# A list scheduler's cost figures are replaced, and with them the order of an attention and MoE kernel

## The chip, the cores and the metric

The kernel runs on one core of one Trainium2 chip. The metric is the device time of one execution in microseconds. A core has five engines that each take their instructions in the order in which the program lists them: TensorE (PE in the profile, its weight loads PEld), VectorE (DVE), ScalarE (ACT), GpSimd (POOL) and SyncE (SP), which here issues all DMAs. An instruction that needs a result of another engine waits for it, and everything behind it on its own engine waits too. So the order within each engine is part of the program.

## The reference

```python
scores = scale * np.matmul(q, k.transpose(0, 1, 3, 2))
log_f = np.log(np.clip(f, 0.0001, 1.0))
cum = np.cumsum(log_f, axis=-1)
decay = cum[:, :, :, None] - cum[:, :, None, :]
scores = np.where(causal, -1000000000.0, scores + decay)
scores = scores - np.max(scores, axis=-1, keepdims=True)
attn = np.exp(scores)
attn = attn / (np.sum(attn, axis=-1, keepdims=True) + 1e-09)
attn_out = np.matmul(attn, v)            # 8 batches, 8 heads, 576 rows, 64 columns
x = attn_out.transpose(0, 2, 1, 3).reshape(4608, 512)
h = np.maximum(np.maximum(x @ w1, x @ w2), x @ w3)      # 4608 x 768
out = h @ w_out                                          # 4608 x 512
```

All inputs are float32, but the kernel takes q, k, v and f as such and the four weight matrices as 64-bit numbers, which it converts on the chip.

## The kernel before

**Heads.** The 64 heads (8 batches of 8) go one after the other. Scores are held transposed, keys on the partitions. A head's 576 query columns are cut into unit 2 (columns 0 to 255) and unit 1 (columns 256 to 575); in the first batch unit 1 is cut again into "a" and "b". `scores(n, unit)` is a chain over four engines. A first pass of matmuls writes the scores into PSUM (banks `s`, L606). From head 16 on VectorE adds the causal mask (L635, L640). ScalarE copies the first block (L671), VectorE takes the maximum over the key blocks (`mx`, L659 to L664), GpSimd reduces it over the partitions (`gm`, L674) and writes the result into a row of the query tile (`qs_r`, L681). A second pass of matmuls (L606 again) adds minus that maximum and the low parts of q and k to the same banks. Then ScalarE takes the exponential (`pf`, L688).

**Split numbers.** To keep float32 accuracy at a faster matmul rate, each factor is split into a high part, rounded by ScalarE, and a low part, subtracted by VectorE. For the weights of the values these are `ph` (L694) and `pl` (L695), and `split_values` runs three groups of matmuls: `ph` with the high values, `ph` with the low ones, `pl` with the high ones (bank `t`, L709). The first batch works in plain float32 instead.

**MoE.** When a batch is done, its output is divided by the row sums, which go through DRAM, and split (`xh`, `xl`). For each of two column chunks (256 and 320 wide) and six blocks of 128 hidden units `gemm1` (L818) computes three products of 12 matmuls each; ScalarE copies the first into `tm` (L825), VectorE takes the maximum with the other two (L827), and the result is split into `hmh` and `hml`. `gemm2` (L847) multiplies with `w_out`. The matmuls of batch b's MoE are the work that fills TensorE while heads of batch b+1 wait for their maxima.

**Buffers.** There are two sets of query and key tiles, so head n+2's DMAs wait for head n's second pass; the PSUM has four banks for scores, one (`t`) for values and three (`mp`) for the MoE.

**The planner.** Nothing of this is issued as it is written. Each step is given to `add` with an engine, a cost in ns, its function, the keys it reads and writes, and a priority. `emit` then simulates the engines: at each moment the engine that can start first takes, of its steps whose inputs are ready, the one with the best rank (priority less a little for the length of work behind it). `LAG` is the time from one engine's end to another's start, a DMA's transfer is queued behind the others, and `GatedClock` gives TensorE half speed after a stretch of 3413 ns with too little work. The steps are then issued in the order of the simulated starts. So a cost that is too low lets the planner believe that a result is there early, and it places the consumer early on its engine.

**Start.** `warm_up` holds 20 matmuls on an identity matrix. Heads 0 and 1 are transposed by TensorE from tiles `hml` and `hmh` (`turn_head`, L432), the other heads of the first batch by VectorE in groups of four (`load_quad`, L491). The decay row of each head goes by a small DMA into the key tile. 24 weight blocks (`load_weights`, L468 to L478) are converted by ScalarE and VectorE in the first 170 us.

Of the kernel before, what the change touches and what calls it, by code (L numbers as in the profile page):

```python
# [23 lines left out]
class GatedClock:  # L24
# [24 lines left out]
class Plan:  # L49
# [8 lines left out]
    ENGINES = ("PE", "ACT", "DVE", "POOL", "SP")  # L58

# [22 lines left out]
    def emit(self):  # L82
# [22 lines left out]
        while done < n:  # L105
# [30 lines left out]
def mm_cost(cols, m):  # L136
    return max(cols / 2.4 + 3, 107 if m > 65 else 55)


def run_cost(cols):  # L140

    load = [m / 1.2 for _, m in cols[1:]] + [107]
    return sum(max(n / 2.4 + 3, x) for (n, _), x in zip(cols, load))
# [11 lines left out]
def kernel(  # L155
# [52 lines left out]
    plan.parts["pf1"] = [f"pf1/{x}" for x in range(3)]  # L208
    for c in ("mx", "gm", "sg"):
# [39 lines left out]
    NB32 = 1  # L249
    UT = [sb(f"u{i}", [P, S]) for i in range(KT)]  # L250
# [115 lines left out]

    def sums_constants():
# [9 lines left out]
    add("POOL", 1800, constants, w=["const"], prio=-9)  # L377
    add("POOL", 150, lambda: nc.gpsimd.memset(LESS.bitcast(F32), -1.0), w=["less"], prio=-9)
    for i in range(H):
        add("POOL", 480, lambda i=i: first_constants(i), w=[f"qf{i}/2"], prio=-9 + i)  # L380
        add("DVE", 369, lambda i=i: nc.vector.memset(KF[i][64:P, :], 0.0), w=[f"kf{i}/2"], prio=-9 + i)
    add("POOL", 1000, value_constants, w=[f"vn{i}" for i in range(4)], prio=-8)


    def decay():
# [16 lines left out]
        add("DVE", 369, lambda: nc.vector.tensor_scalar(c8, ft[0:H, :], -1.0 / scale, None, op0=ALU.mult),  # L402
# [599 lines left out]
```

## Time and profile before

| | |
|---|---|
| median of 3 runs | 991.08 us (990.32 to 992.14) |
| profiled execution | 992.66 us |
| its span, first to last instruction | 990.9 us |
| mean granted TensorE clock | 0.986 |
| DMA | 112.69 MB, mean 114 GB/s |

The page lists busy time per engine, the span in 40 slices of 24.8 us, and groups of equal instructions. A busy TensorE is counted from a matmul's start to its modelled end, so neighbouring matmuls overlap; the spacing of their starts is what one costs. In a row of the timeline stand the start, the length, engine, line, operation, out<-in, shapes, and in brackets the idle time before it and what ended that. A wait row names the engine and line that waited, what it waited for, the total in us, how often, and the longest. "First to second pass" below means the time from the first to the second group of L606 matmuls of one head and unit.

### The profile page before, as it was taken

The page shows a single profiled execution, that of the slowest core. Times are in us where ns is not written, and L with a number is a line of the kernel's source. Part 1 is how long each engine was busy: PE and PEld are TensorE (multiplying, and loading weights), DVE is VectorE, ACT ScalarE, POOL GpSimd, SP SyncE. Part 2 cuts the span into 40 slices and gives each one's busy share as a digit, 9 for nine tenths or more (in the row PEclk, how much of TensorE's full clock was granted, in tenths as well). Part 3 has the DMA queues.
Part 4 walks back from the last instruction along what each step waited for, and adds up shares of the span by engine and source line. Part 5 has one row for each costly group of instructions (what it writes and reads, how often), then busy time and mean ns, then how long its engine had stood idle before and what let it go on. Part 6 is the DMA issues. An engine that isn't in the chain of part 4 may idle for free.

```text
span 990.9 us, 18561 instructions
## 1 busy us (share of the span) xinstructions
PE 947.8 (96%) x6694; PEld 879.9 (89%) x6694; DVE 678.9 (69%) x1355; ACT 513.0 (52%) x1066; POOL 278.7 (28%) x314
## 2 busy tenths in 40 slices
PE   7999897999999999999999999999999999999998
PEld 4789786998989989899999989898998989899998
DVE  8789898687776785758757686667767686543211
ACT  3476556666555564546545654546555564433111
POOL 5553305233232323233213232323232323210000
PEclk9799799999999999999999999999999999999999
DMA  7882664645444452526354343435445352400000
GB/s 208 197 232 46 169 182 97 179 102 162 111 130 118 106 149 70 152 59 165 90 155 119 92 135 84 135 82 156 108 97 152 81 141 67 119 13 35 1 32 22
DMA packets 97258, 112.69 MB, mean 114 GB/s; under 512 B 54048, under 2 KB 63520, under 8 KB 97168
## 3 DMA queue, kind: packets, MB, share of 16 engines
q1 hardware_dynamic: 97168, 111.52, 42.9%
q8 instruction: 53, 0.87, 0.4%
q14 instruction: 37, 0.30, 0.1%
HBM read 50.15 MB, written 9.86 MB: 61 GB/s over the span
## 4 chain that ended last, share of the span: by engine, by line
PE 64%; DVE 14%; POOL 10%; DMA 5%; issue 4%; SPq 2%; ACT 1%; POOLq 0%; DVEq 0%; ACTq 0%
PE mp L818 35%; PE s L606 10%; PE mp L847 9%; PE t L709 8%; POOL gm L674 6%; DVE mx L664 4%; POOL qs_r L681 3%; DVE hl L491 2%; DMA hl<-in_k_dram 2%; DVE pl_r L695 2%; SPq L533 1%; DMA ks_r<-hl 1%; DVE tm L827 1%; DVE s L635 1%; PE mp L606 1%
## 5 line engine op out<-in xcount | busy, mean ns | idle before, releaser
L818 PE MATMUL mp<-xh_r,w_r 128*128 128x320 f32 (+1 forms) x2160 | 462.7, 297 | 0.6 <-DVE tm L827 0.6
L818 PEld LDWEIGHTS mp<-xh_r,w_r 128*128 128x128 f32 x2160 | 356.7, 188 | 2.5 <-DVE tm L827 1.6
L674 POOL PARTITION_ALL_REDUCE gm<-mx x131 | 172.9, 1323 | 579.2 <-DVE mx L664 363.2
L818 PE MATMUL mp<-xl_r,w_r 128*128 128x320 f32 (+1 forms) x1080 | 319.5, 296 | 0.0
L818 PEld LDWEIGHTS mp<-xl_r,w_r 128*128 128x128 f32 x1080 | 203.2, 188 | 0.3
L827 DVE TENSOR_TENSOR tm<-mp,tm 128x256 f32<-128x256 f32 (+1 forms) x192 | 87.1, 454 | 154.0 <-PE mp L818 131.2
L688 ACT ACTIVATE pf<-s 128x384 f32<-128x384 f32 (+4 forms) x251 | 113.7, 505 | 99.8 <-PE s L606 85.3
L606 PE MATMUL s<-qs_r,ks_r 128*128 128x320 f32 (+4 forms) x784 | 132.5, 290 | 24.9 <-POOL qs_r L681 18.8
L606 PEld LDWEIGHTS s<-qs_r,ks_r 128*128 128x128 f32 (+1 forms) x784 | 114.7, 182 | 44.0 <-POOL qs_r L681 32.2
L695 DVE TENSOR_TENSOR pl_r<-pf,ph_r 128x1216 fp32r<-128x1216 f32 (+1 forms) x112 | 113.1, 1011 | 23.7 <-ACT ph_r L694 23.1
L847 PE MATMUL mp<-w_r,hmh_r 128*128 128x512 f32 (+1 forms) x396 | 123.0, 392 | 0.7 <-DVE w_r L478 0.7
L694 ACT ACTIVATE ph_r<-pf 128x1216 fp32r<-128x1216 f32 (+1 forms) x112 | 97.5, 873 | 24.3 <-PE t L709 23.2
L830 ACT ACTIVATE hmh_r<-tm 128x256 fp32r<-128x256 f32 x96 | 39.8, 415 | 129.0 <-DVE tm L827 129.0
L664 DVE TENSOR_TENSOR mx<-mx,s 128x320 f32<-128x320 f32 (+3 forms) x248 | 92.1, 371 | 9.1 <-ACT mx L671 1.9
L491 DVE STREAM_TRANSPOSE hl<-hl 128x576 f32<-128x576 f32 x64 | 75.7, 1245 | 12.5 <-DMA hl<-in_k_dram 12.5
L847 PEld LDWEIGHTS mp<-w_r,hmh_r 128*128 128x128 f32 x396 | 71.0, 189 | 13.0 <-DVE w_r L478 1.0
L681 POOL CAST qs_r<-gm 1x320 fp32r<-1x320 f32 (+1 forms) x112 | 75.2, 674 | 6.9
L847 PE MATMUL mp<-w_r,hml_r 128*128 128x512 f32 (+1 forms) x198 | 77.1, 389 | 0.0
L709 PE MATMUL t<-ph_r,va_r 128*65 128x64 f32 x392 | 61.8, 274 | 2.4 <-ACT r_r L768 1.9
L709 PE MATMUL t<-pl_r,va_r 128*65 128x64 f32 x392 | 61.3, 272 | 1.6 <-DVE pl_r L695 1.3
L709 PE MATMUL t<-ph_r,vl_r 128*65 128x64 f32 x392 | 61.6, 273 | 0.0
L825 ACT ACTIVATE tm<-mp 128x256 f32<-128x256 f32 (+1 forms) x96 | 39.4, 410 | 42.0 <-PE mp L818 40.3
(186 smaller groups left out, 1150.3 us busy)
## 6 DMA issues: line engine op xcount, KB each, us to landing
qs_r<-hl SPq DMA_DIRECT2D x168, 144.0 KB
ks_r<-hl SPq DMA_DIRECT2D x168, 144.0 KB
hl<-in_q_dram SPq DMA_DIRECT2D x16, 576.0 KB
hl<-in_k_dram SPq DMA_DIRECT2D x16, 576.0 KB
w<-in_moe_w_dram SPq DMA_DIRECT2D x18, 512.0 KB
out_dram<-o_r SPq DMA_DIRECT2D x35, 256.0 KB
r_r<-rdram SPq DMA_DIRECT2D x56, 144.0 KB
vn<-in_v_dram SPq DMA_DIRECT2D x58, 128.0 KB
```

Source lines behind the costliest of these rows:

```text
L491: add("DVE", 669, lambda e=e, tt=tt, xs=xs: nc.vector.transpose(tt[:, e], xs[:, e]), [key + "0"], [key + "1"], prio)
L606: nc.tensor.matmul(bank[bk][0:l.shape[-1], col:col + w], l, rhs(qa, w), start=start and bk not in begun, stop=stop, skip_group_check=True)
L664: nc.vector.tensor_tensor(mt[:, a:a + w], mt[:, a:a + w], bank[bk][:, col:col + w], op=ALU.max)
L674: add("POOL", 185 + 3.43 * nq, lambda: nc.gpsimd.partition_all_reduce(gm, mt, P, bass.bass_isa.ReduceOp.max), [km, km + "a"], [kg], prio)
L681: add("POOL", 100 + 0.83 * nq, lambda: nc.gpsimd.tensor_copy(shift_row(), gm[row:row + 1, :]), [kg], [kx], prio)
L688: add("ACT", act_cost(w), lambda bk=bk, w=w, col=col: nc.scalar.activation(pf[:, col:col + w], bank[bk][:, 0:w], AF.Exp, scale=sc), [kb[bk ...
L694: add("ACT", act_cost(PW[unit]) + 40, lambda: nc.scalar.activation(ph(unit), pf, AF.Copy), [fk], [hk], prio)
L695: add("DVE", dve_cost(PW[unit]), lambda: nc.vector.tensor_tensor(pl(unit), pf, ph(unit).bitcast(F32), op=ALU.subtract), [fk, hk], [lk], prio)
L709: nc.tensor.matmul(t[:D + 1, qa:qa + w], src()[:, j, c, :], pr()[:, col:col + w], start=first and x == 0, stop=last, skip_group_check=True,)
L818: nc.tensor.matmul(m, unit_w(i, fb)[:, w, kt, :], xx, start=kt == 0 and x == 0, stop=kt == KT - 1 and x == 2,)
L827: add("DVE", dve_cost(cn), lambda m=m: nc.vector.tensor_tensor(t, m, t, op=ALU.max), [km, kt_], [kt_], prio)
L847: nc.tensor.matmul(mp[:, 0:cn], l[:, fb, cs], unit_o(fb)[:, r, ds], start=fb == 0 and x == 0, stop=fb == FT - 1 and x == 2,)
```

## The change

Most of the figures that the planner works with are replaced; `LAG` stays. TensorE's cost per column goes from 1/2.4 to 0.4477 ns and is then taken times 0.95; ScalarE and VectorE steps get 30 ns each, GpSimd steps 450 ns, and a DMA's landing 400 ns of room. The two limits of the clock model move. Costs of single steps follow: a memset 605 instead of 369, a transpose 1085 instead of 669, the reduction over partitions 450 + 2.6 instead of 185 + 3.43 ns per column, its copy 130 + 0.9 instead of 100 + 0.83. The warm-up matmuls write the bank `s10` (`SP1[0]`) instead of `mp2`. The keys of the value tiles are cut into three. A new set of functions for heads in plain float32 between `H * NB32` and `NV32` comes along, but `NV32` is set to `H`, so no head takes that way; only `second_constants`, four memsets on GpSimd ahead of the second batch, runs.

```diff
-        self.warm = share > (0.4 if self.warm else 0.65)
+        self.warm = share > (0.34 if self.warm else 0.72)
...
+    ROOM = {"PE": (0.95, 0), "ACT": (1.0, 30), "DVE": (1.0, 30), "POOL": (1.0, 450), "SP": (1.0, 0)}
+    LATE = 400
...
-            end = t + self.steps[i][1]
+            cost = self.steps[i][1] * self.ROOM[e][0] + self.ROOM[e][1]
+            end = t + cost
             if e == "PE":
-                end = clock.run(t, self.steps[i][1], self.steps[i][6])
+                end = clock.run(t, cost, self.steps[i][6])
...
-                end = moved = max(moved, end + 650) + self.steps[i][5]
+                moved = max(moved, end + 650) + self.steps[i][5]
+                end = moved + self.LATE
...
 def mm_cost(cols, m):
-    return max(cols / 2.4 + 3, 107 if m > 65 else 55)
+    return max(0.4477 * cols + 3, 107 if m > 65 else 55)
...
+    for i in range(2):
+        plan.parts[f"va{i}"] = [f"va{i}/{x}" for x in range(3)]
...
+    NV32 = H
...
+    def second_constants():
+        for i in range(2):
+            nc.gpsimd.memset(VF(i)[64:P, :, 4, :], 0.0)
+            nc.gpsimd.memset(VF(i)[:, :, :, D:D + 1], 1.0)
...
-        add("DVE", 369, lambda i=i: nc.vector.memset(KF[i][64:P, :], 0.0), w=[f"kf{i}/2"], prio=-9 + i)
+        add("DVE", 605, lambda i=i: nc.vector.memset(KF[i][64:P, :], 0.0), w=[f"kf{i}/2"], prio=-5.5 + 0.1 * i)
...
-            add("PE", 217, lambda: nc.tensor.matmul(MPS[2].rearrange("p (o x) -> p o x", o=4), ident, z, start=True, stop=True),
-                ["const"], ["mp2"], 90)
+            add("PE", 217, lambda: nc.tensor.matmul(SP1[0].rearrange("p (o x) -> p o x", o=4), ident, z, start=True, stop=True),
+                ["const"], ["sp1/0"], 90)
...
-                add("DVE", 669, lambda e=e, tt=tt, xs=xs: nc.vector.transpose(tt[:, e], xs[:, e]),
+                add("DVE", 1085, lambda e=e, tt=tt, xs=xs: nc.vector.transpose(tt[:, e], xs[:, e]),
...
-        add("POOL", 185 + 3.43 * nq, lambda: nc.gpsimd.partition_all_reduce(
+        add("POOL", 450 + 2.6 * nq, lambda: nc.gpsimd.partition_all_reduce(
...
-        add("POOL", 100 + 0.83 * nq, lambda: nc.gpsimd.tensor_copy(
+        add("POOL", 130 + 0.9 * nq, lambda: nc.gpsimd.tensor_copy(
...
-    add("POOL", 200, split_constants, w=["va0", "va1", "vl"], prio=p)
+    add("POOL", 1200, second_constants, w=["va0", "va1"], prio=p)
...
+        if n == NV32:
+            add("POOL", 1000, split_constants, w=["va0", "va1", "vl"], prio=p)
```

The figures act through the order alone, so it is shown at three places. Lines in the change are numbered by its own file: L671, L688, L694, L825 of before are L707, L725, L731, L868 there.

ScalarE, head 47, unit 1, from the copy of the first block of its maxima (`mx`, in the chain between the passes) to its first exponential (`pf<-s_123`, behind the second pass). Before:

```order
L671 ACTIVATE mx_82<-s_124 128x320
L694 ACTIVATE ph_r<-pf_80 128x1216
L766 ACTIVATE u_90<-t 64x320
L768 ACTIVATE r_r<-t 1x320
L688 ACTIVATE pf_81<-s_126 128x384
L825 ACTIVATE tm_121<-mp_130 128x320
L694 ACTIVATE ph_r<-pf_81 128x384
L766 ACTIVATE u_90<-t 64x256
L768 ACTIVATE r_r<-t 1x256
L688 ACTIVATE pf_80<-s_123 128x512
```

The change:

```order
L707 ACTIVATE mx_82<-s_124 128x320
L873 ACTIVATE hmh_r<-tm_121 128x256
L873 ACTIVATE hdh_r<-tm_121 128x64
L868 ACTIVATE tm_122<-mp_130 128x320
L547 ACTIVATE va_r<-vn_75 128x10x64
L517 ACTIVATE hl<-hl 128x1152
L806 ACTIVATE u_91<-t 65x320
L806 ACTIVATE u_91<-t 65x256
L868 ACTIVATE tm_121<-mp_130 128x320
L517 ACTIVATE hl<-hl 128x1152
L873 ACTIVATE hmh_r<-tm_122 128x256
L725 ACTIVATE pf_80<-s_123 128x512
```

Before, one MoE result (`tm`) is copied between the two; in the change two are, with 36 matmuls of TensorE from one to the next, and the high parts of the head before (`ph_r`) have moved ahead of the copy.

ScalarE again, from head 47's first exponential to its high part. Before:

```order
L688 ACTIVATE pf_80<-s_123 128x512
L688 ACTIVATE pf_80<-s_124 128x384
L688 ACTIVATE pf_80<-s_125 128x320
L495 ACTIVATE hl<-hl 128x1152
L830 ACTIVATE hmh_r<-tm_121 128x256
L830 ACTIVATE hdh_r<-tm_121 128x64
L495 ACTIVATE hl<-hl 128x1152
L825 ACTIVATE tm_122<-mp_130 128x320
L517 ACTIVATE va_r<-vn_75 128x10x64
L830 ACTIVATE hmh_r<-tm_122 128x256
L830 ACTIVATE hdh_r<-tm_122 128x64
L694 ACTIVATE ph_r<-pf_80 128x1216
```

The change:

```order
L725 ACTIVATE pf_80<-s_123 128x512
L725 ACTIVATE pf_80<-s_124 128x384
L725 ACTIVATE pf_80<-s_125 128x320
L725 ACTIVATE pf_81<-s_126 128x384
L731 ACTIVATE ph_r<-pf_80 128x1216
```

Eight other steps stood between the exponentials and the high part; in the change it is one, the exponential of the head's unit 2.

SyncE at the start; `hml` and `hmh` receive head 1's raw keys and queries, `qs`, `ks`, `xh`, `xl` the decay rows. Before:

```order
L336 DMA w_97<-in_moe_w_dram 128x4x256
L336 DMA qs_65<-u_91 1x16x36
L336 DMA qs_66<-u_91 1x16x36
L336 DMA ks_67<-u_91 1x16x36
L336 DMA ks_68<-u_91 1x16x36
L336 DMA xh<-u_91 1x16x36 x2
L336 DMA xl<-u_91 1x16x36 x2
L336 DMA hml<-in_k_dram 96x6x64
L336 DMA hmh<-in_q_dram 96x6x64
```

The change:

```order
L353 DMA w_97<-in_moe_w_dram 128x4x256
L353 DMA hml<-in_k_dram 96x6x64
L353 DMA hmh<-in_q_dram 96x6x64
L353 DMA qs_65<-u_91 1x16x36
L353 DMA qs_66<-u_91 1x16x36
L353 DMA ks_67<-u_91 1x16x36
L353 DMA ks_68<-u_91 1x16x36
```

The two raw loads have moved ahead of the eight decay rows. On TensorE head 1's transposes have likewise moved ahead of head 0's first scores.

More of the change, by code (lines that the diff above doesn't have):

```diff
@@ L136, in mm_cost @@
 def mm_cost(cols, m):
-    return max(cols / 2.4 + 3, 107 if m > 65 else 55)
+    return max(0.4477 * cols + 3, 107 if m > 65 else 55)
 def run_cost(cols):
     load = [m / 1.2 for _, m in cols[1:]] + [107]
-    return sum(max(n / 2.4 + 3, x) for (n, _), x in zip(cols, load))
+    return sum(max(0.4477 * n + 3, x) for (n, _), x in zip(cols, load))
 def act_cost(cols):
@@ L208 @@
     plan.parts["pf1"] = [f"pf1/{x}" for x in range(3)]
+    plan.parts["ph1"] = [f"ph1/{x}" for x in range(3)]
+    plan.parts["ph2"] = ["ph2/0"]
     for c in ("mx", "gm", "sg"):
@@ L282, in VA, with VF @@
         return lazy(f"va{i}", [P, 2, 5, D + 1])
+    def VF(i):
+        return lazy(f"va{i}", [P, 2, 5, D + 1], F32, "f")
     def VL():
@@ L315, in pl, with pg @@
         return lazy(f"pl{u}", [P, PW[u]])
+    def pg(u):
+        return lazy(f"ph{u}", [P, PW[u]], F32, "f")
     def unit_w(i, fb):
@@ L401, in decay @@
         c8 = UT[KT - 1][0:H, :]
-        add("DVE", 369, lambda: nc.vector.tensor_scalar(c8, ft[0:H, :], -1.0 / scale, None, op0=ALU.mult),
+        add("DVE", 540, lambda: nc.vector.tensor_scalar(c8, ft[0:H, :], -1.0 / scale, None, op0=ALU.mult),
             ["pf1"], [f"u{KT - 1}"], DP)
@@ L506, in load_v @@
         vn, kv = VN[i], f"vn{i}"
+        if NB32 * NP <= pi < NV32 // 2:
+            for j in range(2):
+                add("SP", 475, lambda j=j: nc.sync.dma_start(
+                    out=VF(s)[:, j, 0:4, 0:D], in_=src[j, 0:512, :].rearrange("(c p) d -> p c d", p=P)),
+                    [], [f"va{s}/{j}"], prio, 262144 / 360)
+            add("SP", 475, lambda: nc.sync.dma_start(
+                out=VF(s)[0:64, :, 4, 0:D], in_=src[:, 512:S, :].rearrange("h p d -> p h d")), [], [f"va{s}/2"], prio, 300000 / 360)
+            return
         after = [f"kf{2 * pi}"] if b < NB32 else []
@@ L574, in buffers @@
     def buffers(n, unit):
-        return SETS[n % len(SETS) if n < H * NB32 else 0] if unit == 2 else BUFS[unit]
+        if n < H * NB32:
+            return SETS[n % len(SETS)] if unit == 2 else BUFS[unit]
+        bufs = SETS[0] if unit == 2 else BUFS[unit]
+        if n < NV32 and n % 2:
+            bufs = bufs[:3] + (None,) + bufs[4:]
+        return bufs
     def scores(n, unit, prio):
@@ L646, in scores @@
             cost[run] = run_cost(ws)
-            ca = sum(4 * w / 2.4 for w, _ in ws) if first else cost[run]
+            ca = sum(4.04 * w / 2.4 for w, _ in ws) if first else cost[run]
             ca += 65 * mask_pe * sum(x[0] in run for x in diag)
@@ L666, in scores @@
         by_act = n < 0 if unit == 2 else True
-        cm = sum(dve_cost(x[1] * x[4]) for x in d["first"] if not (x[4] == 1 and by_act)) + sum(
+        cm = sum(dve_cost(x[1] * x[4]) + 110 * (x[4] == 3) for x in d["first"] if not (x[4] == 1 and by_act)) + sum(
             dve_cost(x[1]) + 128 for x in d["more"]) - 128 * (by_act and bool(d["more"]))
```

45 lines of the change are left out of this document (26 added, 19 removed).

## The prediction

> **What bounds the kernel now.** I read the page first, then the stretches of the span, then TensorE's waits by stretch, and last one head in order of time.
>
> ```profile
> PE 947.8 (96%) x6694; PEld 879.9 (89%) x6694; DVE 678.9 (69%) x1355; ACT 513.0 (52%) x1066; POOL 278.7 (28%) x314
> PEclk9799799999999999999999999999999999999999
> ```
>
> TensorE is busy for 947.8 of 990.9 us, so 43 us of idle time are all that an order can win, and besides them the slices near the start whose clock digit is 7. The stretches (columns: window, length, busy us of PE, PEld, DVE, ACT, POOL, then granted clock, DMA share, GB/s) show three stages.
>
> ```profile
> 0.00:25.00 25.00, 17.86 (x102) 12.10 (x103) 22.18 (x40) 9.01 (x16) 14.30 (x37) 0.99 0.74 210
> 25.00:100.00 75.00, 72.80 (x500) 64.80 (x500) 65.68 (x122) 46.91 (x107) 35.25 (x51) 0.91 0.62 158
> 100.00:175.00 75.00, 64.83 (x438) 57.49 (x436) 65.19 (x119) 44.41 (x90) 22.00 (x22) 0.91 0.54 146
> 175.00:875.00 700.00, 679.82 (x4901) 638.32 (x4900) 495.33 (x1005) 385.97 (x789) 205.74 (x202) 1.00 0.45 118
> 875.00:991.00 116.00, 112.49 (x763) 107.20 (x761) 30.56 (x74) 26.73 (x65) 1.46 (x2) 1.00 0.06 19
> ```
>
> Up to 175 us VectorE is busy for 153 us, TensorE for 155.5: a start-up in which either can be late. From 175 to 875 VectorE has 200 us to spare, and TensorE idles for 20.2 us. The last stretch is matmuls alone, and its 3.5 us are the final store. The middle stage's waits (us in total, times, longest), for matmuls and then for weight loads:
>
> ```profile
> PE s L606 <- POOL qs_r L681: 17.3, 31, 1.4
> PE s L606 <- DMA qs_r<-hl: 0.7, 1, 0.7
> PE t L709 <- DVE pl_r L695: 0.2, 1, 0.2
> ```
> ```profile
> PEld s L606 <- POOL qs_r L681: 29.0, 42, 1.7
> ```
>
> One cause holds nearly all of it: the second score pass waits for GpSimd, which reduces the row maxima over partitions (L674) and writes them into the query tile (L681). Head 47, later columns, shows the whole chain:
>
> ```profile
> 631.27 0.88 PE L606 MATMUL s<-qs_r,ks_r 128*128 128x320 f32 x5
> 632.17 0.42 DVE L635 TENSOR_TENSOR s<-s,mask 128x256 f32<-128x256 f32 x1
> 633.24 1.26 DVE L491 STREAM_TRANSPOSE hl<-hl 128x576 f32<-128x576 f32 x1 [0.65 <-DMA hl<-in_k_dram]
> 634.34 1.64 DVE L664 TENSOR_TENSOR mx<-mx,s 128x320 f32<-128x320 f32 x4
> 635.90 1.42 DVE L695 TENSOR_TENSOR pl_r<-pf,ph_r 128x1216 fp32r<-128x1216 f32 x1
> 636.15 2.27 POOL L674 PARTITION_ALL_REDUCE gm<-mx  x1 [2.63 <-DVE mx L664]
> 637.72 0.31 PE L818 MATMUL mp<-xh_r,w_r 128*128 128x320 f32 x1
> 638.49 0.87 POOL L681 CAST qs_r<-gm 1x320 fp32r<-1x320 f32 x1
> 639.41 0.91 PE L606 MATMUL s<-qs_r,ks_r 128*128 128x320 f32 x5 [1.38 <-POOL qs_r L681]
> ```
>
> From the first pass's end, 632.15, to the second's start, 639.41, the chain takes 7.3 us; the last matmul placed between them starts at 637.72. Both GpSimd steps are late against the stage's means:
>
> ```profile
> L674 POOL PARTITION_ALL_REDUCE gm<-mx x101 | 138.9, 1378 | 485.1 <-DVE mx L664 308.2 <-DVE mx L661 129.6 <-PE s L606 19.5
> L681 POOL CAST qs_r<-gm 1x320 fp32r<-1x320 f32 x51 | 33.4, 655 | 3.3
> ```
>
> **The change, part by part.** No instruction of TensorE, VectorE, ScalarE or the DMA queue is added or taken away; only the planner's figures change, and with them the order on each engine. So I add up waits.
>
> *The POOL waits of the middle stage.* What decides is how much other TensorE work stands between a head's first and second pass: I call it the cover. I counted it in both orders for all heads 14 to 63 and both column parts, pricing each matmul by the trace's spacing:
>
> ```profile
> 633.45 0.46 PE L818 MATMUL mp<-xh_r,w_r 128*128 128x320 f32 x2
> 633.74 0.31 PE L818 MATMUL mp<-xl_r,w_r 128*128 128x320 f32 x1
> 633.89 0.45 PE L818 MATMUL mp<-xh_r,w_r 128*128 128x320 f32 x2
> ```
>
> Three 320-wide matmuls start in 0.44 us, 147 ns each. For head 47's later columns 45 matmuls stand between the passes before (5.9 us) and 71 in the change (9.5 us; 48 of them 320-wide, 7.1 us). Over the 50 heads the later columns go from a mean of 5.9 to 8.9 us, smallest 7.6 from head 16 on; the first 256 columns from 5.4 to 9.4, smallest 7.7. The chain needs 7.3 us when as late as in head 47. Without the transpose that ran ahead of the maxima (1.26) and with GpSimd near its means (2.27 to 1.38, 0.87 to 0.66) it is 4.9. So almost every cover now exceeds the chain, with some 4 us over the usual one. What a stall costs lies between the two wait rows: in head 47 the matmul before started at 637.72, the next could at 637.87 and did at 639.41, a loss of 1.54 between 1.38 and 1.65, the latter being what the load row counts. I take 26 of the 29.0 for all, and leave 2 for the few covers that a very late GpSimd step eats: **-24**, bounds -15 (17.3 less 2) and -29.
>
> *What the cover is taken from.* The second pass now stands nearer to the weighted values. For the later columns the cover from the second pass to the first value matmul falls from a mean of 14.9 to 3.6 us (smallest 2.8), and to the matmuls that need the low part from 16.7 to 5.2 (smallest 4.6). The need, from head 47:
>
> ```profile
> 640.10 1.31 ACT L688 ACTIVATE pf<-s 128x512 f32<-128x512 f32 x3 [3.03 <-PE s L606]
> 640.16 0.31 PE L818 MATMUL mp<-xh_r,w_r 128*128 128x320 f32 x1
> 634.98 0.49 ACT L688 ACTIVATE pf<-s 128x384 f32<-128x384 f32 x1
> 635.37 0.43 ACT L825 ACTIVATE tm<-mp 128x320 f32<-128x320 f32 x1
> 648.38 1.22 ACT L694 ACTIVATE ph_r<-pf 128x1216 fp32r<-128x1216 f32 x1 [0.34 <-PE t L709]
> ```
>
> TensorE goes on at 640.16; the exponentials end at 641.41, 1.25 later. The changed ScalarE order puts the other part's exponential next (0.39, start to start) and then the high part (1.22): 2.9 us, against 3.6. VectorE's 1.42 for the low part makes 4.3, against 5.2. It fits with 0.7 to 0.9 to spare, and with nothing at the smallest covers. I take **+3**, 0.06 per head; bounds 0 and +10, which is 0.2 us in each of 50 heads.
>
> *The start-up.* Two effects meet. Head 1's raw keys and queries leave ahead of the eight decay rows instead of behind them:
>
> ```profile
> 10.15 1.22 SPq L336 DMA_DIRECT2D qs<-u  x2
> 14.04 0.89 PE L606 MATMUL s<-qs 128*128 128x256 f32 x4 [0.54 <-ACT qs L439]
> 15.27 0.52 SPq L336 DMA_DIRECT2D hml<-in_k_dram  x1
> 18.07 1.20 PE L432 MATMUL mp<-tm,hml 96*64 96x96 f32 x12 [0.53 <-DMA hml<-in_k_dram]
> ```
>
> The rows wait for their data until 10.15, so two issues ahead of them (0.52 for the first, the second alike) cost nothing. In the trace the load was issued at 15.27 and its transposes ran 2.8 us later; issued some 5 us earlier, behind the first weights, it lets them run at about 13 (an estimate from this distance). But TensorE's order now puts them ahead of head 0's scores, which started at 14.04. The warm-up matmuls write another bank, so the fourth transpose of head 0 stands with the other three; the 20 warm-ups cost what they did. Then VectorE sets the pace: priced by the trace, its steps up to those that head 11 needs are 9.7 us more than TensorE's work up to there before, 9.1 in the change. That floor stays. What can move is VectorE's own idle time, 22 us of the first 175. I take **-2**, bounds -12 (half of it) and +10 (as much lost again).
>
> The clock is part of it. Its rows:
>
> ```profile
> 100.00:125.00 25.00, 20.60 (x128) 18.32 (x126) 21.64 (x44) 14.11 (x29) 7.75 (x10) 0.80 0.62 172
> 103.31 0.28 PE L818 MATMUL mp<-pl_xa,w_r 128*128 128x256 f32 x1
> 105.74 0.65 PE L606 MATMUL s<-qs_r,ks_r 128*128 128x320 f32 x4 [2.15 <-issue]
> ```
>
> A pause of 2.15 us is followed by a clock of 0.80 over this stretch; over 25 to 175 us it is 0.91, 13.5 us lost. I keep that loss, for the floor keeps the pauses. The Trainium skill, "TensorE: Matmul & The Clock Gate", section "HAM oscillation — how this bites in real kernels", puts the limit at pauses of more than about 3.4 us. By that rule a start-up with pauses like this one's would run at full clock; the rows above say otherwise, and the sum goes by them.
>
> *Nothing.* `second_constants` adds four memsets on GpSimd. The nearest rows are of the same sizes, 0.20 and 0.12:
>
> ```profile
> 3.45 0.20 POOL L359 MEMSET vn<- 64x130 f32 x1
> 3.71 0.12 POOL L360 MEMSET vn<- 128x10 f32 x1
> ```
>
> Together 0.64 us at the start of batch 1, behind a wait for head 7's values that GpSimd already had there; if uncovered, head 8 waits 0.64.
>
> **Sum:** -24 + 3 - 2 = -23 us on a span of 990.9, so 968. The profiled execution took 992.66 in all, 1.76 around its span; the median of the runs is 991.08. I predict the median: **968 us**. The corners are 991 - 41 = 950 and 991 + 5 = 996.
>
> **The rivals.**
>
> *A, start-up gains too (955).* VectorE's idle time closes and head 1 is early: -12 more. For: 22 us of VectorE idle; against: the floor of 9 us is as before.
>
> *B, full clock in the start-up (954).* If only long pauses bring half speed, the 13.5 us go as well. For: the stage is a chain of pauses below 2.2 us; against: its clock is 0.91. The skill's page named above is this rule.
>
> *C, half of the POOL waits stay (980).* The chain grows with the cover: both parts' reductions now follow each other on GpSimd, and VectorE may put more work ahead of the maxima. The transpose in head 47 shows how. Against: it would take 4 us in every other head. -24 becomes -12.
>
> *D, the start-up loses (982).* Head 0's scores stand behind head 1's transposes and weights come later; +14 by the bound above and some clock.
>
> *E, slower (about 1000).* The place is the value matmuls of the later columns. ScalarE and VectorE run behind by more than the 0.7 to 0.9 us left, in every head, because each high or low part sits behind one more step (0.43 for a copy, 1.26 for a transpose). Against -26 elsewhere it decides from 26/50 = 0.52 us of wait per head on; at 0.7 it is +35, less 26: 1000. For: the high part was late before as well, at 648.38, seven us after its exponentials. Against: that was its place in the order.
>
> *F, no change (991).* The orders differ but the waits return in the same sum. Against: no cover of the 100 is now below the usual chain.
>
> **Numbers.** Forecast 0.50 (own range 960 to 976), A 0.13, B 0.03, C 0.14, D 0.10, E 0.07, F 0.03. The range 953 to 984 leaves out E, F and tails of the others. This kernel tells 0.2%, 2 us, from nothing. Faster: forecast, A, B, C and nearly all of D, 0.89; same 0.04, F and a rest; slower 0.07, E.
>
> **What would show it.** Right: between 175 and 875 us TensorE idles for 4 us or less, the rows "PE s <- POOL qs_r" come to under 3 us, and "PE t" waits for VectorE or ScalarE appear, small. First step wrong: those POOL rows stay above 8 us. Second: the "PE t" rows pass 10 us. Third: at the start of head 16's scores the changed kernel is over 8 us ahead or behind once the POOL waits are set aside. A clock below 1.00 after 200 us would upset all of it.

## The result and the profile after

The changed kernel takes 960.04 us (median of 4 runs, 958.37 to 960.95), the kernel before 990.7 us beside it: a ratio of 0.969, 95% interval 0.967 to 0.972. The forecast was 968 us with a range of 953 to 984. The profiled execution took 958.37 us in all, with a span of 956.6 against 990.9.

The page of the changed kernel, busy time and the clock's slices:

```profile
PE 931.5 (97%) x6694; PEld 879.2 (92%) x6694; DVE 674.3 (70%) x1355; ACT 501.4 (52%) x1066; POOL 253.2 (26%) x318
PEclk7999999999999999999999999999999999999999
```

The stretches of the changed kernel (window, length, busy us and count of PE, PEld, DVE, ACT, POOL, then clock, DMA share, GB/s):

```profile
0.00:25.00 25.00, 18.79 (x103) 14.11 (x104) 19.36 (x36) 8.33 (x14) 12.92 (x35) 0.80 0.75 211
25.00:100.00 75.00, 66.76 (x464) 58.98 (x463) 69.99 (x124) 45.40 (x102) 36.78 (x52) 0.93 0.72 189
100.00:175.00 75.00, 69.44 (x512) 64.85 (x511) 67.25 (x123) 48.91 (x101) 24.86 (x30) 0.95 0.45 125
175.00:875.00 700.00, 698.37 (x5085) 666.53 (x5085) 500.63 (x1033) 384.33 (x814) 178.60 (x204) 1.00 0.46 118
875.00:957.00 82.00, 78.18 (x540) 74.72 (x538) 17.11 (x42) 14.46 (x37) 0.00 (x0) 1.00 0.06 20
```

The middle stage shows the gain. In the same 700 us TensorE starts 5085 matmuls instead of 4901 and idles for 1.6 us instead of 20.2. The 184 more are 25 us of work at 698.37/5085 = 0.137 us each. Up to 175 us it has done 1079 instead of 1040, some 6 us. What is left behind 875 us takes 82 us instead of 116. GpSimd needs less time in the stage as well: 178.60 us instead of 205.74 for the same kind of work. The traces show where. The row of the copies before gives shortest, median and longest (ns):

```profile
L681 POOL CAST qs_r<-gm x101: 396/450/1507, 177.4 to 868.9; 1x320 fp32r<-1x320 f32 x51, 1x256 fp32r<-1x256 f32 x50
```

Of these 101 copies 20 run mostly beside VectorE's subtraction for the low part (`pl_r`, L695) and take 0.87 to 1.50 us each; the 15 that run beside no VectorE step take 0.40 to 0.45. In the change none of the 102 copies runs mostly beside that subtraction, and of the reductions 10 do instead of 25 (1.6 to 1.85 us each in the change, against 1.06 to 1.14 with VectorE idle). No run changes this alone.

The waits of that stage, matmuls and then weight loads (us in total, times, longest):

```profile
PE mp L861 <- DVE tm L870: 1.3, 1, 1.3
```
```profile
PEld mp L861 <- DVE tm L870: 1.5, 1, 1.5
PEld t L746 <- DVE pl_r L732: 0.6, 2, 0.4
PEld s L642 <- POOL qs_r L717: 0.3, 1, 0.3
```

The query row, for which weight loads waited 29.0 us in 42 places, is waited for once, 0.3 us. The value matmuls (`t`) wait for 0.6 us.

Head 47 again, GpSimd and then TensorE's passes, in order of time:

```profile
633.12 1.40 POOL L710 PARTITION_ALL_REDUCE gm<-mx  x1 [8.65 <-DVE mx L700]
634.90 1.63 POOL L710 PARTITION_ALL_REDUCE gm<-mx  x1 [0.38 <-PE t L746]
636.60 0.80 POOL L717 CAST qs_r<-gm 1x320 fp32r<-1x320 f32 x2
```
```profile
628.02 0.99 PE L642 MATMUL s<-qs_r,ks_r 128*128 128x320 f32 x7
638.24 0.99 PE L642 MATMUL s<-qs_r,ks_r 128*128 128x320 f32 x7
```

The rows of the two parts are now written together (x2), behind both reductions, and end at 637.40. The second pass starts at 638.24 with no idle time ahead of it, 0.84 us later. Before, it started at 639.41 after waiting 1.38 us.

### The profile page after: what moved, and what is told of

Same layout as the page of the kernel before. It is cut to its first block, busy times and chain, and to the rows that moved or that the text cites. A ratio compares the mean times of both kernels' runs of the same rounds, so it can differ in the third digit from the quotient of the medians.

```text
span 956.6 us, 18333 instructions
## 1 busy us (share of the span) xinstructions
PE 931.5 (97%) x6694; PEld 879.2 (92%) x6694; DVE 674.3 (70%) x1355; ACT 501.4 (52%) x1066; POOL 253.2 (26%) x318
## 4 chain that ended last, share of the span: by engine, by line
PE 86%; DVE 3%; DMA 1%; ACT 1%; issue 1%; SPq 0%; DVEq 0%; ACTq 0%
PE mp L861 47%; PE mp L890 15%; PE t L746 14%; PE s L642 10%; DVE pl_r L732 1%; DMA rdram<-sc 0%; DVE mx L700 0%; DMA r_r<-rdram 0%; DVE hl L519 0%; PE t L782 0%; DMA ks_r<-hl 0%; DMA qs_r<-hl 0%; ACT pf L725 0%; DVE ph L778 0%; PE s L658 0%
## 5 line engine op out<-in xcount | busy, mean ns | idle before, releaser
L861 PE MATMUL mp<-xh_r,w_r 128*128 128x320 f32 (+1 forms) x2160 | 475.7, 298 | 1.5 <-DVE tm L870 1.3
L710 POOL PARTITION_ALL_REDUCE gm<-mx x131 | 165.5, 1289 | 586.1 <-DVE mx L700 531.9
L725 ACT ACTIVATE pf<-s 128x384 f32<-128x384 f32 (+2 forms) x251 | 108.8, 508 | 69.0 <-PE s L642 63.7
L642 PE MATMUL s<-qs_r,ks_r 128*128 128x320 f32 (+4 forms) x784 | 120.8, 283 | 3.9 <-DMA ks_r<-hl 2.4
L731 ACT ACTIVATE ph_r<-pf 128x1216 fp32r<-128x1216 f32 (+1 forms) x112 | 97.1, 887 | 3.7 <-PE t L746 3.5
L868 ACT ACTIVATE tm<-mp 128x256 f32<-128x256 f32 (+1 forms) x96 | 39.7, 414 | 60.0 <-PE mp L861 57.5
L676 DVE TENSOR_TENSOR s<-s,mask 128x64 f32<-128x64 f32 x48 | 11.3, 235 | 80.8 <-PE s L642 80.6
```

The lines of the kernel that those rows point to most:

```text
L642: nc.tensor.matmul(bank[bk][0:l.shape[-1], col:col + w], l, rhs(qa, w), start=start and bk not in begun, stop=stop, skip_group_check=True)
L710: add("POOL", 450 + 2.6 * nq, lambda: nc.gpsimd.partition_all_reduce(gm, mt, P, bass.bass_isa.ReduceOp.max), [km, km + "a"], [kg], prio)
L725: add("ACT", act_cost(w), lambda bk=bk, w=w, col=col: nc.scalar.activation((pg(unit) if pk else pf)[:, col:col + w], bank[bk][:, 0:w], AF. ...
L731: add("ACT", act_cost(PW[unit]) + 40, lambda: nc.scalar.activation(ph(unit), pf, AF.Copy), [fk], [hk], prio)
L861: nc.tensor.matmul(m, unit_w(i, fb)[:, w, kt, :], xx, start=kt == 0 and x == 0, stop=kt == KT - 1 and x == 2,)
```

## Experiments

For the runs below I use three numbers per head and part, as means over heads 14 to 63. The **need** is the time in the trace from the end of the first pass to the end of GpSimd's copy of that head's row. The **cover** is the work placed between the passes, counted in the order and priced as in the prediction. The **margin** is cover minus need. "Load waits" are the waits of TensorE's weight loads. Each ratio is to the kernel before on the same chip, with its 95% interval.

### Which figures make the gain

*The GpSimd figures alone, on the kernel before.*

```diff
-            end = t + self.steps[i][1]
+            end = t + self.steps[i][1] + (450 if e == "POOL" else 0)
-        add("POOL", 185 + 3.43 * nq, lambda: nc.gpsimd.partition_all_reduce(
+        add("POOL", 450 + 2.6 * nq, lambda: nc.gpsimd.partition_all_reduce(
-        add("POOL", 100 + 0.83 * nq, lambda: nc.gpsimd.tensor_copy(
+        add("POOL", 130 + 0.9 * nq, lambda: nc.gpsimd.tensor_copy(
```

> The kernel before with the change's GpSimd figures alone: 450 + 2.6 and 130 + 0.9 ns per column, and 450 ns of room for each GpSimd step. Theory (the cover between the passes makes the gain, and the GpSimd figures make the cover): counted in its order, the covers of heads 14 to 63 have means of 7.0 us (first 256 columns) and 7.7 (later columns) against 5.4 and 5.9 before and 9.4 and 8.9 in the change. With needs of 4.3 and 5.65 us, the two that reproduce the waits of before, only 0.1 us is missing in all (19.1 before). So the waits of TensorE and its weight loads for the query row after 175 us fall below 2 us, some 27 us are won, and the start-up stays as before: 964 us (960 to 968). Rival 1 (the TensorE figures or the whole set is needed): 980 or more. Rival 2 (with covers of 5 us left in many heads the waits come back in half): 975.

Measured: 970.5 us, ratio 0.977 (0.975 to 0.980). Waits of the weight loads, 175 to 875 us:

```profile
PEld s L606 <- POOL qs_r L681: 4.0, 5, 1.1
```

25 of the 29.0 us of load waits for the query row go with these figures alone, and 4 us of them stay where I had expected under 2; the time is a little above my range. The profiled execution ends 17.8 us behind the changed kernel's; 9.5 of that are the start-up, and the rest lies behind it (both below).

*The GpSimd figures put back in the changed kernel.*

```diff
-    ROOM = {"PE": (0.95, 0), "ACT": (1.0, 30), "DVE": (1.0, 30), "POOL": (1.0, 450), "SP": (1.0, 0)}
+    ROOM = {"PE": (0.95, 0), "ACT": (1.0, 30), "DVE": (1.0, 30), "POOL": (1.0, 0), "SP": (1.0, 0)}
-        add("POOL", 450 + 2.6 * nq, lambda: nc.gpsimd.partition_all_reduce(
+        add("POOL", 185 + 3.43 * nq, lambda: nc.gpsimd.partition_all_reduce(
-        add("POOL", 130 + 0.9 * nq, lambda: nc.gpsimd.tensor_copy(
+        add("POOL", 100 + 0.83 * nq, lambda: nc.gpsimd.tensor_copy(
```

> The changed kernel with the three GpSimd figures put back to those of before (185 + 3.43, 100 + 0.83, no room), all else as changed. Theory: covers fall to means of 6.1 and 6.7 us; by the same needs 12.1 us are missing, 0.63 of before's 19.1, so 0.63 x 29 = 18 us of the load waits return: 978 us (972 to 982), and the waits for the query row after 175 us come to 10 to 19 us. Rival 1 (the gain is the other figures'): 960 to 963. Rival 2 (all of it returns): 987 or more.

Measured: 967.3 us, ratio 0.975 (0.972 to 0.977). The same wait row:

```profile
PEld s L642 <- POOL qs_r L717: 6.1, 14, 0.8
```

A miss, in none of the three ranges: 6 us of waits come back, not 18. The other figures take most of the waits away without GpSimd's. I had held the need of each head fixed, but it differs from head to head by 1 to 2 us (standard deviation), and the planner follows it: cover and need agree head by head with correlations of 0.78 to 0.97 in the first four runs and in both kernels. So I looked at the margin from here on.

*TensorE's figures alone, on the kernel before.*

```diff
-        self.warm = share > (0.4 if self.warm else 0.65)
+        self.warm = share > (0.34 if self.warm else 0.72)
-                end = clock.run(t, self.steps[i][1], self.steps[i][6])
+                end = clock.run(t, 0.95 * self.steps[i][1], self.steps[i][6])
-    return max(cols / 2.4 + 3, 107 if m > 65 else 55)
+    return max(0.4477 * cols + 3, 107 if m > 65 else 55)
...
```

> The kernel before with the change's TensorE figures alone (0.4477 ns per column, 4.04 passes for plain float32, the factor 0.95, the two limits of the clock model). Theory: covers of 5.0 and 5.8 us, a little less than before (5.4 and 5.9); 25.7 us are missing by the needs against 19.1, so waits of 29 x 25.7 / 19.1 = 39 us instead of 29: 1001 us (991 to 1006), the start-up being another order by some us. Rival 1 (a planner that knows TensorE's time better wins): 975 or less.

Measured: 1001.25 us, ratio 1.010 (1.006 to 1.013), and

```profile
PEld s L606 <- POOL qs_r L681: 32.2, 44, 2.8
```

They win nothing by themselves; the waits grow a little, by 3 us where I expected 10.

*The figures of VectorE and ScalarE put back in the changed kernel.*

```diff
-    ROOM = {"PE": (0.95, 0), "ACT": (1.0, 30), "DVE": (1.0, 30), "POOL": (1.0, 450), "SP": (1.0, 0)}
+    ROOM = {"PE": (0.95, 0), "ACT": (1.0, 0), "DVE": (1.0, 0), "POOL": (1.0, 450), "SP": (1.0, 0)}
-        add("DVE", 605, lambda i=i: nc.vector.memset(KF[i][64:P, :], 0.0), w=[f"kf{i}/2"], prio=-5.5 + 0.1 * i)
+        add("DVE", 369, lambda i=i: nc.vector.memset(KF[i][64:P, :], 0.0), w=[f"kf{i}/2"], prio=-9 + i)
-                add("DVE", 1085, lambda e=e, tt=tt, xs=xs: nc.vector.transpose(tt[:, e], xs[:, e]),
+                add("DVE", 669, lambda e=e, tt=tt, xs=xs: nc.vector.transpose(tt[:, e], xs[:, e]),
...
```

> The changed kernel with the figures of VectorE and ScalarE put back (no 30 ns of room, memset 369 and early, transpose 669, scan 669 and so on). Head 1's transposes stand behind head 0's scores again. Theory: covers of 7.0 and 7.4 us on the mean, nothing missing by the needs, so the middle stage stays without waits for GpSimd (below 2 us) and the kernel keeps 27 of the 31 us won. The start-up: the wait of 4.6 us for head 1's raw keys goes, the later gain of it may go as well: 955 to 966. Rival 1 (the transposes' figure is what makes the cover): 975 or more. Rival 2 (the gain of 5 us in the start-up hangs on these figures): 965.

Measured: 965.6 us, ratio 0.973 (0.971 to 0.976). The wait for the query row stays away, but other waits are above it now:

```profile
PEld mp L861 <- DVE tm L870: 3.2, 5, 1.2
PEld s L642 <- ACT pf L725: 2.7, 3, 1.2
PEld t L746 <- DVE pl_r L732: 2.5, 3, 1.4
PEld s L642 <- POOL qs_r L717: 1.4, 2, 1.2
```

The time lies in my range, but not by my theory: the start-up is better than the changed kernel's, and the stage behind it worse (below).

*Both sets put back:* TensorE's figures, the 400 ns for transfers, the bank and the memsets are left. Beside the lines of the two runs above:

```diff
-    ROOM = {"PE": (0.95, 0), "ACT": (1.0, 30), "DVE": (1.0, 30), "POOL": (1.0, 450), "SP": (1.0, 0)}
+    ROOM = {"PE": (0.95, 0), "ACT": (1.0, 0), "DVE": (1.0, 0), "POOL": (1.0, 0), "SP": (1.0, 0)}
```

> The changed kernel with the figures of GpSimd and those of VectorE and ScalarE put back; left are TensorE's figures, the 400 ns for transfers, the warm-up bank and the four memsets. After the first four runs the theory is new: the planner tracks the need of each head well (need = first pass's end to the reduction's end, and 0.8 us for the copy), and what counts is the margin of cover over need. Its mean is 0.0 us (first 256 columns) and 0.3 (later columns) before, 2.6 and 2.9 in the change, 1.6 and 1.7 with the GpSimd figures alone, 0.7 and 0.8 with all but these; with a spread of some 0.7 us, half a microsecond more takes most waits away. So either set of figures is enough. Theory: with both put back the covers are 5.2 and 5.9 us, as before; margin about 0, 25 to 32 us of load waits for the query row: 990 us (985 to 996). Rival (what is left of the change gives the rest, as a better knowledge of TensorE's time): 975 or less.

Measured: 990.7 us, ratio 0.999 (0.996 to 1.001), and

```profile
PEld s L642 <- POOL qs_r L717: 25.3, 41, 1.7
```

So the gain lies in these two sets together, and for the waits for the query row either is nearly enough.

*One number on the kernel before.*

```diff
-           "POOL": (200, 75, 46, 96, 75), "SP": (1173, 908, 950, 983, 950)}
+           "POOL": (1100, 75, 46, 96, 75), "SP": (1173, 908, 950, 983, 950)}
```

> The kernel before with one number changed: the planner's time from a GpSimd step's end to a TensorE step's start is 1100 ns instead of 200. No step's cost is touched. Theory (any margin will do, wherever it is put): covers of 6.2 and 7.4 us, margin 0.8 to 1.4, load waits for the query row after 175 us of 1 to 6 us: 970 us (964 to 976), most of the change's gain from one number. Rival (the true cost of each step is needed, since the need differs from head to head): above 980.

Measured: 972.8 us, ratio 0.977 (0.970 to 0.985), and

```profile
PEld s L606 <- POOL qs_r L681: 2.9, 5, 1.0
```

No step's cost is any truer than before, and 26 of the 29 us of waits are gone. For this wait it is enough that the second pass is placed about a microsecond later than the planner thinks necessary.

### How much margin there is

*Each reduction issued twice from head 14 on,* in the changed kernel and in the one before, with unchanged orders:

```diff
-        add("POOL", 450 + 2.6 * nq, lambda: nc.gpsimd.partition_all_reduce(
-            gm, mt, P, bass.bass_isa.ReduceOp.max), [km, km + "a"], [kg], prio)
+        add("POOL", 450 + 2.6 * nq, lambda: [nc.gpsimd.partition_all_reduce(
+            gm, mt, P, bass.bass_isa.ReduceOp.max) for _ in range(2 if n >= 14 else 1)], [km, km + "a"], [kg], prio)
```

> The changed kernel in its own order, but from head 14 on each reduction over partitions is issued twice (the second gives the same result). The need grows by one reduction, 1.2 us (first 256 columns) and 1.4 (later columns), more where one part's reduction stands behind the other's. Theory: with margins of 2.6 and 2.9 us that stays hidden: 960 to 966. Rival (GpSimd's steps are no longer what TensorE would wait for only because they became faster, with no room left): 100 x 1.3 = 130 us more, above 1020.

> The kernel before with the same doubling. Theory: with margins of 0.0 and 0.3 us each doubled reduction is waited for: 100 x 1.3 = 130 us as a bound, less where one wait covers the other part's: 1050 to 1120. Rival (the waits of before come from something else that GpSimd only ends last): 990 to 1010.

Measured: 994.3 us for the changed kernel, ratio 1.001 (0.999 to 1.004), and 1086.4 us for the kernel before, ratio 1.092 (1.081 to 1.103). The wait rows, of the changed kernel and then of the one before:

```profile
PEld s L642 <- POOL qs_r L717: 32.5, 47, 1.9
```
```profile
PEld s L606 <- POOL qs_r L681: 101.0, 72, 3.3
```

The first was a miss by 30 us, and GpSimd's order in time in head 47 tells why:

```profile
656.82 5.03 POOL L710 PARTITION_ALL_REDUCE gm<-mx  x4 [6.43 <-DVE mx L700]
661.92 1.87 POOL L717 CAST qs_r<-gm 1x320 fp32r<-1x320 f32 x2
```

All four reductions run before the first row is copied, so doubling costs each head two of them, not one: the needs go from 7.0 and 6.9 us to 9.4 and 9.2. And the margin was smaller than I had written: I had measured it to the reduction's end and added 0.8 us; to the end of the head's own copy it is 2.4 and 1.9. Less 2.3 to 2.4 that is nothing, and the waits are those of the kernel before, which has no margin either. The table holds both kernels and the runs up to here, with margins to the copy's end (first 256 columns / later columns):

| kernel | need us | cover us | margin us | load waits us, 175 to 875 | ratio |
|---|---|---|---|---|---|
| before, reductions twice | 6.9 / 7.0 | 5.4 / 5.9 | -1.5 / -1.1 | 101.0 | 1.092 |
| change, reductions twice | 9.4 / 9.2 | 9.4 / 8.9 | 0.0 / -0.3 | 32.5 | 1.001 |
| before, TensorE's figures | 5.2 / 5.7 | 5.1 / 5.8 | -0.1 / 0.1 | 32.2 | 1.010 |
| before | 5.3 / 5.6 | 5.4 / 5.9 | 0.1 / 0.3 | 29.0 | 1 |
| change, both sets back | 5.1 / 5.6 | 5.2 / 5.9 | 0.1 / 0.3 | 25.3 | 0.999 |
| change, GpSimd's back | 5.4 / 5.9 | 6.1 / 6.7 | 0.7 / 0.8 | 6.1 | 0.975 |
| before, one number | 5.2 / 6.1 | 6.2 / 7.4 | 1.1 / 1.3 | 2.9 | 0.977 |
| before, GpSimd's figures | 5.4 / 6.3 | 7.0 / 7.7 | 1.6 / 1.4 | 4.0 | 0.977 |
| change, VectorE's back | 5.4 / 6.0 | 7.0 / 7.4 | 1.6 / 1.4 | 1.4 | 0.973 |
| change | 7.0 / 6.9 | 9.4 / 8.9 | 2.4 / 1.9 | 0.3 | 0.969 |

The margins of single heads spread by 0.4 to 1.3 us around these means. With the mean near zero 42 of the 100 second passes wait (29.0 us); at 0.7 it is 14; beyond 1 us there is little left to win of this wait.

The rest of the time hangs on the other waits. Behind the start-up (from the moment that the section on it defines to the end of the span) the kernels differ as the sums of all their load waits do:

| kernel | load waits for the query row, us | all load waits, us | us behind the start-up |
|---|---|---|---|
| before | 29.0 | 34.5 | 807.9 |
| change, VectorE's back | 1.4 | 14.4 | 789.2 |
| before, one number | 2.9 | 13.7 | 788.1 |
| before, GpSimd's figures | 4.0 | 12.9 | 787.0 |
| change, GpSimd's back | 6.1 | 8.3 | 782.6 |
| change | 0.3 | 3.7 | 778.7 |

More cover without the figures of VectorE and ScalarE leaves 9 to 13 us of other waits, where before had 5.5; with these figures it is 2 to 3.4. So this set is worth some 10 us behind the start-up, though hardly any of it shows in the row of the query.

*Twice the room,* in the changed kernel:

```diff
-    ROOM = {"PE": (0.95, 0), "ACT": (1.0, 30), "DVE": (1.0, 30), "POOL": (1.0, 450), "SP": (1.0, 0)}
+    ROOM = {"PE": (0.95, 0), "ACT": (1.0, 30), "DVE": (1.0, 30), "POOL": (1.0, 900), "SP": (1.0, 0)}
```

> The changed kernel with 900 ns of room for each GpSimd step instead of 450. Covers of 10.3 and 9.8 us on the mean, but 0.7 to 3 us in a few heads, where no other work was left to place: by the old needs 10.6 us are missing there. Theory (margin saturates: beyond 2 us there is nothing left to take away, and cover is taken from elsewhere): 964 to 972, with 4 to 10 us of waits for the query row in a few heads. Rival (more room is better still): below 958.

Measured: 997.6 us, ratio 1.005 (1.003 to 1.007), far beyond what I had expected. The mean margin is 3.5 and 2.8 us, and the load waits of the middle stage are

```profile
PEld s L642 <- ACT pf L725: 9.0, 6, 2.6
PEld s L642 <- POOL qs_r L717: 4.6, 1, 4.6
PEld t L746 <- ACT ph_r L731: 2.6, 3, 1.0
PEld mp L861 <- ACT o_r L897: 2.4, 4, 0.8
```

GpSimd is waited for once, but now ScalarE is: first passes wait for banks whose exponentials (`pf`) are late. The start-up suffers too:

```profile
25.00:50.00 25.00, 15.70 (x68) 12.58 (x65) 16.99 (x29) 7.76 (x17) 5.49 (x5) 0.54 1.10 246
```

TensorE is busy for 15.7 of these 25 us, at a clock of 0.54. At the moment that the next section defines, 9.9 us are lost to the changed kernel; the profiled spans differ by 40.8, so most is lost behind it, part of it from 240 to 290 us, where the one long wait for the query row ends and the clock is 0.91. My reading of the first heads, which no run tests, is that a planner which gives every small GpSimd step 0.9 us finds no other work for TensorE in the first heads, and spaces them out. Of the three rooms that were run, 0 (with the old costs of the reduction and the copy), 450 and 900 ns, the middle one is the fastest; they place the best no closer.

### The start-up

To compare start-ups I take the moment at which TensorE has done the first 145 us of its work, priced at undisturbed spacing and counted in each order. It is 183.0 us before and 177.9 in the change. Each such moment comes from one execution, and executions of one kernel differ: those with the GpSimd figures alone took 968.3 to 976.2 us at granted clocks of 0.993 to 0.981, and the profiled one is the longest. So differences of a few us between these moments need not be the order's.

*The wait for head 1's raw keys filled.* In the first 36 us of the changed kernel matmuls wait for

```profile
PE mp L454 <- DMA hml<-in_k_dram: 4.6, 1, 4.6
PE s L642 <- DMA ks<-hl: 1.6, 1, 1.6
```

```diff
-        for _ in range(20):
-            add("PE", 217, lambda: nc.tensor.matmul(...),
+        for x in range(20):
+            add("PE", 217, lambda x=x: [nc.tensor.matmul(...)
+                                        for _ in range(1 + (x >= 6) + (x >= 14))],
```

> The changed kernel in its own order, but of its 20 warm-up matmuls the last 14 are issued twice and the last six of these a third time: 20 more on the same bank, 0.23 us each, 4.6 us in the place where TensorE waited 4.55 us for head 1's raw keys. What the kernel computes is the same. Theory (the half clock from 12.5 to 22.7 us follows that wait, and costs 5.1 us of work): the clock stays full up to 25 us, and 955 us (953 to 958) if the stage that follows keeps the gain. Rival (the floor of the start-up is VectorE's, as the forecast had it: TensorE's faster steps wait for it a little later): the clock is full there, but 959 to 962.

Measured: 960.0 us, ratio 0.967 (0.965 to 0.969): no gain that this can tell, as the rival had it. The stretches, first of the changed kernel, then with the wait filled:

```profile
12.50:22.70 10.20, 7.86 (x38) 7.19 (x39) 6.59 (x14) 2.79 (x5) 1.15 (x1) 0.50 0.60 125
25.00:38.30 13.30, 10.85 (x71) 8.64 (x69) 12.98 (x22) 6.25 (x14) 5.92 (x10) 0.87 1.02 245
```
```profile
12.50:22.70 10.20, 8.45 (x68) 7.04 (x66) 9.13 (x20) 3.18 (x6) 3.60 (x5) 1.00 0.67 139
22.70:25.00 2.30, 1.72 (x13) 1.04 (x12) 1.72 (x4) 0.87 (x2) 2.30 (x5) 0.93 0.98 309
25.00:38.30 13.30, 9.72 (x38) 8.39 (x38) 9.24 (x13) 4.90 (x10) 2.66 (x4) 0.50 1.02 244
```

The clock is full where it was half, and half where it was nearly full. In the filled run head 0's scores start 2 us earlier, and then TensorE meets the next late transfer:

```profile
PE s L643 <- DMA ks<-hl: 3.6, 1, 3.6
```

That wait is 2 us longer than in the changed kernel and ends at 28.91 us instead of 29.37. The DMA share is 1.02 in this stretch in both. By these rows the transfers, and not VectorE as the rival had it, are the floor there, and what is saved ahead of it is given back. At 145 us of work the filled run stands at 179.4.

*VectorE's figures put back in the first batch alone,* so that head 1's transposes stand behind head 0's scores again (the memsets and the steps of the decay as before, and):

```diff
-                add("DVE", 1085, lambda e=e, tt=tt, xs=xs: nc.vector.transpose(tt[:, e], xs[:, e]),
+                add("DVE", 669 if b < NB32 else 1085, lambda e=e, tt=tt, xs=xs: nc.vector.transpose(tt[:, e], xs[:, e]),
```

> The changed kernel with the figures of VectorE put back in the first batch alone (memsets 369 and early, the decay's steps, its transposes 669): head 1's transposes stand behind head 0's scores again, and the rest of the order keeps covers of 8.9 and 8.6 us. Theory: margins stay near 2 us, so the stage after 175 us loses no more than the change does; the start-up is that of the kernel with all VectorE figures put back, which lost 3.4 us less up to the same work: 957 (954 to 962). Rival (the start-up turns on chance; the kernel with the GpSimd figures alone has nearly the same first steps and lost 9 us more than the change): 966 or more.

Measured: 964.2 us, ratio 0.972 (0.970 to 0.974), between my range and the rival's. The margins are 2.4 and 2.1 us and the middle stage has no row of waits for the query row. The first wait has only changed its name, in the first 36 us:

```profile
PE s L642 <- DMA qs<-u: 3.5, 1, 3.5
```

Here head 0's scores wait for the decay rows instead, which the queue issues in the other order. 145 us of work are done at 180.2 us.

*The warm-up matmuls back on their bank,* in the changed kernel:

```diff
-            add("PE", 217, lambda: nc.tensor.matmul(SP1[0].rearrange("p (o x) -> p o x", o=4), ident, z, start=True, stop=True),
-                ["const"], ["sp1/0"], 90)
+            add("PE", 217, lambda: nc.tensor.matmul(MPS[2].rearrange("p (o x) -> p o x", o=4), ident, z, start=True, stop=True),
+                ["const"], ["mp2"], 90)
```

> The changed kernel with the warm-up matmuls back on the bank mp2. Theory: the bank itself is worth nothing, but the order of the whole shifts with it: head 0's fourth transpose waits for the end of the warm-ups, and the covers fall from means of 9.4 and 8.9 us to 7.7 and 8.1. Margins near 1 us: load waits for the query row of 1 to 4 us, and 960 to 966. Rival (the bank frees TensorE early in the start-up): 968 or more.

Measured: 967.0 us, ratio 0.974 (0.973 to 0.976). Middle stage and clock:

```profile
175.00:875.00 700.00, 698.05 (x5111) 666.49 (x5111) 508.19 (x1034) 391.10 (x821) 189.87 (x208) 1.00 0.46 118
```

A miss: the margins are 2.1 and 1.7 us, not near 1, for the needs fell with the covers, and the stage is as full as in the change. All of the loss is in the start-up, where 145 us of work are done at 187.3 us. The prediction costed this edit at nothing.

Over the runs with other first steps that moment lies between 174.6 (VectorE's figures put back) and 187.8 us (room of 900 ns): 187.4 with the GpSimd figures alone, 182.7 with them put back, 183.9 with the one number. The clock accounts for a part: over the first 175 us it is 0.95 with VectorE's figures put back, 0.92 before and in the change, 0.90 with the GpSimd figures alone and 0.88 with room of 900 ns, and 0.01 of it is 1.75 us. It does not account for the bank, with 0.92. Beyond that the runs don't show a rule. My reading, which no run tests, is that a small difference in the figures re-sorts the first heads' steps, and that their place in the full transfer queue then costs or wins some us either way.

## Why the prediction was right or wrong

*What bounds the kernel: right.* The waits for the query row were the loss, as the doubled reductions and the one-number edit show from both sides. But "43 us of idle time are all that an order can win" was wrong. TensorE's idle time fell by 18 us, from 43.1 to 25.1, and its busy time by 16.3, from 947.8 to 931.5, for the same matmuls. Part of a wait stands in the busy column: loads waited 29.0 us and matmuls 17.3 for the same rows, and the difference of 11.7 us lies within the 16.3.

*The POOL waits, -24: mechanism right, size short.* The load row fell from 29.0 to 0.3. I left 2 us for covers that a late GpSimd step eats, and took 26 of 29 for all; neither was needed. The measured term lies between -25 (the 184 matmuls) and -29 (the row), at the far end of my bounds. What made head 47's two GpSimd steps late, the subtraction beside them, has moved away for most heads, which I had not foreseen. My reason was loose in one place: "some 4 us over the usual" chain. Rival C's mechanism happened: both reductions follow each other, and the need rose from 5.3 and 5.6 us to 7.0 and 6.9. The cover rose by 4.0 and 3.0, so a margin of some 2 us is left, half of what I counted.

*The value matmuls, +3: over-sized.* The wait rows of `t` add up to 0.6 us. The covers of 3.6 and 5.2 us against needs of 2.9 and 4.3 were enough in all heads but two. Rival E had the same place and did not occur in the change.

*The start-up, -2: right sign, -5 measured* (183.0 against 177.9; 39 more matmuls by 175 us say 6). Head 1's transposes started at 14.84 us where I had estimated 13, after TensorE had waited 4.55 us for the keys; head 0's scores began at 18.84 instead of 14.04. That was made good later. "VectorE sets the pace: that floor stays" was half right. A floor it is, since filling the wait won nothing, but at 29 us it is the transfers, not VectorE. That the sign came out is partly luck: with other first steps the moment lies anywhere from 8.4 us ahead of the kernel before to 4.8 behind it.

*The clock: right in size, in part by luck.* I kept its loss as it was. The half-clock stretches of the start-up add up to 27 us in both kernels, 13.6 us lost; but they lie elsewhere in the change, and in other orders they add up to as little as 17 and as much as 41 us. The rows from 25 us on are better (0.93 and 0.95 against 0.91 twice) only because 10.2 us of them lie ahead of that. The Trainium skill, "TensorE: Matmul & The Clock Gate", section "HAM oscillation — how this bites in real kernels", speaks of pauses above about 3.4 us. The trace does not agree: in the filled run the clock is half from 24.7 us on (0.93 over 2.3 us is 0.3 us at half), the pause of 3.6 us begins behind that, at 25.3, and no pause between two matmuls up to then is above 1.1 us. The Trainium skill, same page, section "A second HAM failure mode: psum-queue depth-cycling", says of a kernel that cycles through PSUM banks that frequent micro-idles between groups of matmuls made the clock oscillate. The pauses here are of that short kind, 0.6, 1.1 and 0.6 us in these first 25 us, but they are only three. In the trace TensorE is busy for 1.78 of the 3.40 us from 21.20 to 24.60, just ahead of the half clock; which share or pause sets it off, no run tests.

*Nothing for the bank: wrong by its way, not by itself.* The 20 matmuls cost the same, but the bank is a key of the planner; with the old one the order is another and by the ratios 5 us longer (0.974 against 0.969).

The sum: -29, 0 and -5 make the 34 us of the span (5.1 up to 145 us of work, 29.2 behind); I had -24, +3 and -2. All three errors have one sign. What was to show it came out: idle time 1.6 us (4 allowed), query rows 0.3 (under 3), and head 16's first scores start at 212.8 us before and 213.0 after (within 8). The small waits of `t` that were to appear are 0.6 us of load waits; the matmuls have no such row.

GpSimd's steps in the middle stage became shorter on the mean (reductions 1378 to 1315 ns, copies 664 to 492): the long ones beside VectorE's subtraction are fewer, as shown above. Left open is how much of the kernel's time that is worth, and what of the start-up could be won by a chosen order: its half-clock stretches, 27 us, are still in the changed kernel.

## What to carry to other kernels

Where engines run in the order of a plan, compare cover with need head by head and ask for the margin: at a mean margin near zero four second passes in ten wait, one microsecond on a chain of 5 to 7 removes nine tenths of that wait, and it matters little which figure supplies it. Then add up the waits of all other rows, for a cover taken without true costs elsewhere left 9 to 13 us of them here. More margin is not better: with 900 ns of room the exponentials came late, the first heads stood apart, and the gain was gone. An edit that costs nothing as an instruction can still move a plan; when only an order changes, read its cost from the order and the trace, not from the edit.

## What the runs showed of the hardware

- The half clock moves rather than goes. With the 4.55 us wait filled by matmuls, 12.5 to 22.7 us ran at 1.00 instead of 0.50, and 25 to 38.3 us at 0.50 instead of 0.87.
- GpSimd's reductions back to back take 5.03 us for four, 1.26 us each, of 256 and 320 columns, where one of them took 2.27 us in the kernel before.
- A one-row copy on GpSimd took 0.40 to 0.45 us with VectorE idle and 0.87 to 1.50 us beside VectorE's subtraction of two tiles (`pl_r`), in the kernel before.
- The share of busy time hides waiting: the same 6694 matmuls were busy for 929.7 to 965.9 us in these runs, most where loads waited most (965.9 with 101.0 us of load waits).
